# Weight conversion of a two-stage fp32 kernel: a low word's part added in PSUM and a range count on TensorE, fillers in three sizes, a written-out rank for every task

## The chip, the cores and the metric

The kernel runs on one core of one Trainium2 chip. The metric is the device time of one execution in microseconds (us); lower is better. Times of several runs are given as a median with the lowest and the highest.

## The reference

A linear attention without softmax is followed by a two-layer network with a softplus between the layers. All inputs are float32 but the two weights of the network, which come as float64.

```python
kv  = einsum('bhsd,bhse->bhde', k, v)          # 8 batches, 8 heads, s = 576, d = 64
out = einsum('bhsd,bhde->bhse', q, kv)
out = out / sqrt(mean(out * out, axis=-1) + 1e-6) * g_norm
x   = out.transpose(0, 2, 1, 3).reshape(4608, 512)
h   = x @ w_in                                 # 512 x 2048
y   = (maximum(h, 0) + log1p(exp(-abs(h)))) @ w_out   # 2048 x 512
```

## The kernel before

**Precision.** The big products run on TensorE in the reduced type float32r. So each operand (activations x, weights, softplus outputs g) is split into three factors: a high part, the rest scaled by 4096, and a third that corrects their product. Three matmuls then stand for one product. ScalarE makes the high part, VectorE the rest and, for x and g, the third.

**Weights.** The float64 weights arrive as pairs of 32-bit words. `weight` (L410 to L477) takes 512 KB at a time: `c` counts 16 chunks of the 2048 hidden units, and each chunk has an input weight (even j) and an output weight (odd j). VectorE builds a float32 from the high word (`high1` L433, `high2` L437), `mask` (L442) clears what is out of range by help of a square that ScalarE made (L429), `power` (L450) and `rest` (L455) turn the low word into a small float32, and `total` (L459) adds the two. ScalarE's `beyond` (L446) sums how many elements were in range into a column of `over`, from which `whole_scale` derives the scale of the output at L1173. `split_weight` (L486) then makes the three factors: `high` (L496 or L498), `low` (L503 or L506), `low_up` (L509), and for the first four chunks, whose eight weights are needed at once, the third factor goes by TensorE: two matmuls with the identity and the negative identity (`less_by_pe`, L520 and L521) into a PSUM bank, and ScalarE's `third_of_bank` (L524) reads it.

**Attention.** `kv_of` multiplies k and v (small matmuls of 64x64, L691), `rows` turns q on TensorE (L771) or VectorE (L746), multiplies it by kv (L715), squares the result on ScalarE (L788), sums it on VectorE (L719), takes the inverse root on GpSimd (L723), and scales (L727). The first twelve of 36 token tiles are turned by TensorE (L733), the others by VectorE; the first six are split into factors at once (`split`, L635, L638, L641), the others go through DRAM and come back.

**Network.** In the first part a step takes 384 tokens and one chunk: 12 matmuls of 384 columns into a bank (`mm1`, L858), softplus and factors (L880, L882, L869, L873), and nine matmuls of 512 columns for the second layer (`mm2`, L865). In the second part wide steps of 512 tokens take two chunks at once by a scheme with seven products in place of eight (L1060) and 24 matmuls of the second layer (L1130).

**Order.** Nothing of the order is left to a framework. Every piece of work is a task with an engine, an assumed duration, the tasks it follows, buffers it takes and gives back (rings such as `h`, two PSUM banks, `m`, eight SBUF tiles, `raw` and `rawb`, one buffer each for arriving weights), and a due position `pos`. `Plan.order` goes through an assumed time: at each turn it takes, among the tasks that could start soonest, the one with the lowest position, and writes it at the end of its engine's instructions. HANDOVER, READY, SWITCH and LANDING are its assumptions on hand-offs, first starts, changes between kinds of matmuls, and DMAs. Where it foresees at least 400 ns without work for TensorE before the seventh step, it puts a filler there (`warm`, L1224): a matmul of the identity with itself over 512 columns, into a bank of ring `h`, whose result nobody reads. SyncE (SP) issues the DMAs in the order in which the plan lists them.

Of the kernel before, what the change touches and what calls it, by code (L numbers as in the profile page):

```python
# [23 lines left out]
E = 1.0 / RADIX  # L24

# [30 lines left out]
class Plan:  # L56
# [4 lines left out]
    HANDOVER = {"PE": 250, "ACT": 120, "DVE": 120, "POOL": 150, "SP": 0}  # L61
    READY = {"PE": 2500, "ACT": 2500, "DVE": 4000, "POOL": 2500, "SP": 700}
    SWITCH = {("all", "rows"): 90, ("all", "kv"): 90, ("rows", "all"): 250, ("kv", "all"): 250, ("rows", "kv"): 140, ("kv", "rows"): 140}
    TOGETHER, PATIENCE = 1, 0.0
    LANDING, FILLED = 3500, 60000
    KEEP = 4
    BEGIN = 4000
    SOON = 150

# [9 lines left out]
    def add(self, engine, ns, run, after=(), pos=0.0, take=(), give=(), size=0, behind=None, follows=None, kind="all"):  # L79
        pos, behind = round(pos, 4), None if behind is None else round(behind, 4)  # L80
        t = Task(engine, ns, run, [a for a in after if a is not None], pos, list(take), list(give), size)
        for s in t.give:
            s.readers += 1
        self.tasks.append(t)
        t.follows = follows
        t.behind = behind
        t.kind = kind
        return t

    def order(self):  # L90
# [30 lines left out]
        dma_free = 1500  # L121
        last_read = {}
        kind = "all"
        done, left = [], len(self.tasks)
        while left:
            best = None
            for engine, tasks in ready.items():
                options = []
                for t in tasks:
                    at = max(engine_free[engine], t.ready)  # L130
                    if t.size:
                        at = max(at, dma_free - 2500)
# [22 lines left out]
                if engine == "PE" and self.spare and self.spare[-1].start is None:  # L155
                    ring, run, ns, _ = self.spare
                    begin = max(engine_free["PE"], self.BEGIN, min(free[ring])[0] if free[ring] else at)
                    if begin + ns <= at:
                        s = Slot(ring)
                        at, t = begin, Task("PE", ns, lambda s=s: run(s), [], None, [s], [s], 0)  # L160
                        t.kind = "all"
                        s.readers = 1
# [14 lines left out]
            if t.engine == "PE":  # L177
                t.ns += self.SWITCH.get((kind, t.kind), 0)
                kind = t.kind
            t.start = at  # L180
            engine_free[t.engine] = at + t.ns
            t.end = at + t.ns + self.HANDOVER[t.engine]
            if t.size:
                dma_free = max(dma_free, at + t.ns) + t.size
                t.end = dma_free + (self.LANDING if dma_free > self.FILLED else 2000)
# [16 lines left out]
def kernel(  # L202
# [80 lines left out]
    const.tile([P, 8], F32, name="gap0")  # L283
# [125 lines left out]
    def weight(j, pos, fetch_pos, behind):  # L409

        c, of_out = divmod(j, 2)
        raw, w = slot("rawb" if j % 2 and c < 8 else "raw"), slot("m")
        words = 2 if wide else 1
# [7 lines left out]
        f = add("SP", 450, fetch, (), fetch_pos, [raw], size=1800, behind=behind)  # L421
        if wide:
# [30 lines left out]
            def rest():  # L453
                pf = p.tile.bitcast(F32)
                nc.vector.scalar_tensor_tensor(out=pf, in0=words_of()[0], scalar=2.0 ** -52, in1=pf,  # L455
                                               op0=ALU.mult, op1=ALU.mult)

# [7 lines left out]
            d3 = add("DVE", 690, mask, [d2, a1], pos, [])  # L465
            over_done.append(add("ACT", 910, beyond, [d3], pos + (4 if c < 4 else 0), [], [sq]))
# [6 lines left out]
        if c < OWN:  # L473
            divide(j, w, ready, pos, c < 4)
# [4 lines left out]
    def divide(j, w, ready, pos, by_pe=False):  # L479
# [4 lines left out]
        factors_done[of_out, c] = split_weight(w, lambda x: x, d_model, dst, [ready], pos, not of_out, by_pe)  # L484

    def split_weight(w, part_of, n, dst, ready, pos, of_in, by_pe=False):  # L486
# [31 lines left out]
        def less_by_pe():  # L518
            y = new(bank, [P, n])
            nc.tensor.matmul(y, lhsT=ident_r, rhs=dst.tile[:, 0], start=True, stop=False)  # L520
            nc.tensor.matmul(y, lhsT=minus_r, rhs=dst.tile[:, 1], start=False, stop=True)  # L521

        def third_of_bank():
            nc.scalar.activation(dst.tile[:, 2], bank.tile, func=AF.Copy, scale=-E / (1.0 + E))  # L524

# [3 lines left out]
        if by_pe:  # L529
            bank = slot("h")  # L530
            e = add("ACT", 640, low_up, [b], pos, [], [d])
            b2 = add("PE", 500, less_by_pe, [e], pos, [bank])
            e2 = add("ACT", 600, third_of_bank, [b2], pos, [], [bank])
            return [a, e, e2]
# [68 lines left out]
    def load_q(b):  # L603
# [13 lines left out]
        for a in range(4):  # L617
            for p in range(0, NP, 2):
                q_loads[b].append(add("SP", 500, lambda a=a, p=p: run(a, p), (), pos + 0.1 * (2 * a + p // 2),
                                      [q_slots[b]] if not (a or p) else [], [], 1095, behind=pos - 3.5,  # L620
                                      follows=q_loads[b][-1] if a or p else None))

    def split(t, x, ready, pos):
# [20 lines left out]
        a = add("ACT", 640, high, [ready] + ([] if i == 0 else [first_high[n]]), pos, [dst] if i == 0 else [])  # L644
# [17 lines left out]
    def kv_of(b):  # L662
# [7 lines left out]
        for p in range(NP + 1):  # L670
# [4 lines left out]
            def load(src, s, p=p, tail=tail, n=n, ks=ks):  # L675
                if tail:
# [6 lines left out]
                       650 if tail else 850, behind=pos - 5.5) for of_v, (src, s) in enumerate(((k, ks), (v, vs)))]  # L683
# [11 lines left out]
            last = add("PE", 470, run, lds + ([last] if b < 2 else []), pos + 0.5 * p, [bank] if p == 0 else [], [ks, vs], kind="kv",  # L695
# [3 lines left out]
        kv_ready[b] = [add("ACT", 400, lambda: nc.scalar.copy(kvs[b % 2], bank.tile), [last] + o_tasks.get(b - 2, []),  # L699
                           pos + 2.5, [], [bank])]  # L700

    def rows(t):
# [38 lines left out]
        for b, r0, n, s0 in parts(t):  # L741
# [32 lines left out]
            ld = add("SP", 900, load, (), pos - EARLY[7] + P7[20 + t], [q_s] if not at_qa or t == 0 else [], [], 1220 * n // P,  # L774
                     behind=pos - 3.5, follows=first_load[0] if t and at_qa else None)
            first_load.append(ld)
            a = add("PE", 440, turn_q, [ld], pos - 1, [tp], [q_s])
# [482 lines left out]
```

## Time and profile before

| | |
|---|---|
| median of 3 runs | 868.56 us (868.41 to 869.19) |
| span of the profiled execution | 867.5 us |
| TensorE busy | 853.9 us in 6464 matmul records |
| VectorE busy | 704.4 us, 995 instructions |
| ScalarE busy | 521.3 us, 980 instructions |
| GpSimd busy | 76.6 us, 79 instructions |
| first matmul of the network (L858) starts | 44.44 us |
| fillers (L1224) | 52 |
| granted TensorE clock, mean | 1.000 |

A matmul of plain float32 stands in the trace as two records, one of float32r as one. The busy time of a group of matmuls is no measure of what one of them costs, since they overlap; the distance from one start to the next is. All times in the views are from the first instruction of the profiled execution.

### The profile page before, as it was taken

To read this page: it belongs to the slowest core of one execution; us is meant where nothing else is said; L and a number is where in the kernel's file an instruction comes from. 1 tells how busy PE (TensorE), PEld (TensorE's weight loads), DVE (VectorE), ACT (ScalarE), POOL (GpSimd) and SP (SyncE) were. 2 spreads that over 40 slices of the span, in tenths; PEclk is the share of its full clock that TensorE was granted. 3 is DMA by queue.
4 is the path that set the end of the run, shared out by engine and by line. 5 is a ranking of instruction groups with operands and counts; after the bars stand their busy time and mean duration, and the time that the engine had idled before them with its cause. 6 is when DMAs were issued, how large, how long until landed. Compare 5 with 4: busy or idle time off the path is not lost.

```text
span 867.5 us, 17041 instructions
## 1 busy us (share of the span) xinstructions
PE 853.9 (98%) x6464; PEld 760.3 (88%) x6464; DVE 704.4 (81%) x995; ACT 521.3 (60%) x980; POOL 76.6 (9%) x79
## 2 busy tenths in 40 slices
PE   7899999999999999999999999999999999999998
PEld 5678888898888999989999999998999899999996
DVE  7888898888788879798887798878788666788873
ACT  6866664445444467766667655654868555566654
POOL 0342223111113200000000000000000000000000
PEclk9999999999999999999999999999999999999999
DMA  9998998779773655436645546545364752777764
GB/s 278 285 242 230 244 262 255 172 224 234 211 188 114 180 175 166 145 108 209 210 156 164 168 151 205 188 144 170 122 201 140 230 165 91 241 236 241 242 190 126
DMA packets 239778, 167.07 MB, mean 193 GB/s; under 512 B 106320, under 2 KB 198736, under 8 KB 239696
## 3 DMA queue, kind: packets, MB, share of 16 engines
q1 hardware_dynamic: 239392, 165.86, 64.5%
q8 instruction: 50, 0.82, 0.4%
q14 instruction: 32, 0.26, 0.1%
q10 hardware_dynamic: 304, 0.13, 0.1%
HBM read 112.98 MB, written 52.95 MB: 191 GB/s over the span
## 4 chain that ended last, share of the span: by engine, by line
PE 94%; DVE 1%; ACT 1%; POOL 0%; issue 0%; ACTq 0%; DVEq 0%
PE banks L1130 31%; PE banks L1060 28%; PE banks L865 16%; PE banks L858 15%; PE banks L715 2%; PE banks L691 2%; PE banks L733 0%; DVE units L638 0%; DVE half L727 0%; PE banks L1224 0%; POOL roots L723 0%; DVE units L641 0%; DVE roots L719 0%; DVE m L459 0%; ACT units L635 0%
## 5 line engine op out<-in xcount | busy, mean ns | idle before, releaser
L1130 PE MATMUL banks<-pieces,gv 128*128 128x512 f32 x768 | 239.9, 394 | 0.0
L1130 PEld LDWEIGHTS banks<-pieces,gv 128*128 128x128 f32 x768 | 133.5, 189 | 18.4
L1130 PE MATMUL banks<-pieces,g_False 128*128 128x512 f32 x384 | 149.4, 389 | 0.0
L858 PE MATMUL banks<-units,pieces 128*128 128x384 f32 x768 | 145.4, 337 | 0.0
L865 PE MATMUL banks<-pieces,gv 128*128 128x512 f32 x576 | 144.9, 396 | 0.0
L858 PEld LDWEIGHTS banks<-units,pieces 128*128 128x128 f32 x768 | 135.5, 188 | 4.8
L865 PEld LDWEIGHTS banks<-pieces,gv 128*128 128x128 f32 x576 | 106.1, 188 | 20.3
L1060 PEld LDWEIGHTS banks<-units,pieces 128*128 128x128 f32 x840 | 112.8, 190 | 6.8 <-ACT banks L1105 0.4
L1060 PE MATMUL banks<-units,pieces 128*128 128x256 f32 x840 | 117.1, 282 | 0.0
L880 ACT ACTIVATE half<-banks 128x384 f32<-128x384 f32 x64 | 31.4, 491 | 98.2 <-PE banks L858 98.0
L1120 DVE TENSOR_TENSOR gv<-g_True,gv 128x1024 fp32r<-128x1024 f32 x47 | 57.5, 1223 | 37.8 <-ACT gv L1117 37.8
L1130 PEld LDWEIGHTS banks<-pieces,g_False 128*128 128x128 f32 x384 | 72.2, 188 | 15.9
L1060 PEld LDWEIGHTS banks<-units,w 128*128 128x128 f32 x504 | 67.8, 190 | 3.9 <-ACT banks L1105 0.2
L1060 PE MATMUL banks<-units,w 128*128 128x256 f32 x504 | 70.7, 282 | 0.0
L723 POOL TENSOR_TENSOR roots<-roots,half 128x8 f32<-128x8 f32 x36 | 62.3, 1731 | 3.0
L1123 DVE SCALAR_TENSOR_TENSOR g_False<-gv 128x1024 fp32r<-128x1024 f32 x47 | 57.6, 1225 | 1.5
L1109 DVE TENSOR_TENSOR g_True<-banks,g_True 128x512 f32<-128x512 f32 x48 | 33.1, 690 | 30.5 <-PE banks L1060 24.5
L1087 ACT ACTIVATE g_True<-banks 128x256 f32<-128x256 f32 x96 | 36.6, 382 | 32.8 <-PE banks L1060 32.2
L1023 DVE TENSOR_TENSOR units<-loads,units 128x1024 fp32r<-128x1024 f32 x42 | 51.2, 1219 | 6.3 <-ACT units L1020 6.3
L925 ACT ACTIVATE m<-banks 128x512 f32<-128x512 f32 x72 | 42.1, 595 | 19.8 <-PE banks L1130 13.8
L1026 DVE SCALAR_TENSOR_TENSOR units<-units 128x1024 fp32r<-128x1024 f32 x42 | 51.4, 1224 | 1.8
L869 DVE TENSOR_TENSOR gv<-half,gv 128x384 fp32r<-128x384 f32 x64 | 35.4, 553 | 20.6 <-ACT gv L882 19.9
(115 smaller groups left out, 1260.5 us busy)
## 6 DMA issues: line engine op xcount, KB each, us to landing
loads<-x SPq DMA_DIRECT2D x180, 128.0 KB, 2.6
part<-m SPq DMA_DIRECT2D x72, 256.0 KB, 2.9
m<-part SPq DMA_DIRECT2D x72, 256.0 KB, 3.2
loads<-form SPq DMA_DIRECT2D x45, 256.0 KB, 3.2
form<-loads SPq DMA_DIRECT2D x36, 256.0 KB, 3.0
raw<-in_moe_w_in_dram SPq DMA_DIRECT2D x16, 512.0 KB, 4.5
loads<-in_k_dram SPq DMA_DIRECT2D x32, 256.0 KB, 4.1
loads<-in_v_dram SPq DMA_DIRECT2D x32, 256.0 KB, 4.4
```

The source lines that it names most:

```text
L723: nc.gpsimd.tensor_tensor(out=r.tile, in0=r.tile, in1=half, op=ALU.pow)
L858: nc.tensor.matmul(hp, lhsT=w_in.tile[:, i, kd * P:(kd + 1) * P], rhs=xv.tile[:, i, kd], start=(m == 0), stop=(m == 3 * KD - 1))
L865: nc.tensor.matmul(mine[i].tile, lhsT=gv.tile[:, m, i * P:(i + 1) * P], rhs=w_out.tile[:, m], start=(c == cs[0] and m == 0), stop=(c == cs ...
L869: nc.vector.tensor_tensor(out=gv.tile[:, 1], in0=g.tile, in1=gv.tile.bitcast(F32)[:, 0], op=ALU.subtract)
L925: a = add("ACT", 690 if ph == LAST else 600, lambda: nc.scalar.activation(new(ot, [P, d_model]), bank.tile, func=AF.Copy, scale=scale if p ...
L1023: nc.vector.tensor_tensor(out=part_of(1, F32R), in0=xl.tile if m > 1 else xl.tile[:, 0], in1=part_of(0), op=ALU.subtract)
L1026: nc.vector.scalar_tensor_tensor(out=part_of(2, F32R), in0=part_of(1), scalar=-RADIX, in1=part_of(0), op0=ALU.mult, op1=ALU.add)
L1060: nc.tensor.matmul(place(q), lhsT=w[:, m, at:at + P], rhs=dst.tile[:, m, v, kd] if u < 6 else dst.tile[:, m, kd], start=(u == 0 and not m ...
L1087: nc.scalar.activation(dst, src, func=AF.Softplus, scale=1.0 + E)
L1120: nc.vector.tensor_tensor(out=gvt(1, F32R), in0=gt(), in1=gvt(0), op=ALU.subtract)
L1123: nc.vector.scalar_tensor_tensor(out=gt(F32R), in0=gvt(1), scalar=-RADIX, in1=gvt(0), op0=ALU.mult, op1=ALU.add)
L1130: nc.tensor.matmul(mine[i].tile, lhsT=(gvt(m, F32R) if m < 2 else gt(F32R))[:, c, i * P:(i + 1) * P], rhs=outs[c].tile[:, m], start=fresh ...
```

## The change

Four things change.

1. For the first eight weights, `total` is gone. The high factor and the rest `low` are made from the high word's value `t` alone, while the low word's part is written to a buffer of its own (`low_word`, already multiplied by the norm's gain where it is an input weight). TensorE adds the rest and the low word's part in a PSUM bank with two matmuls by the identity. ScalarE's `low_up` reads that bank; the third factor goes by TensorE as before.
2. For the same weights `beyond` is gone. TensorE counts: four matmuls of one column, with the squares as the stationary operand and a tiny constant as the moving one, into a bank; ScalarE reads its one column into `over`.
3. Fillers come in three sizes, 512, 256 and 128 columns, put where the plan foresees 270, 160 or 100 ns without work.
4. The positions are no longer those of the formulas: a list RANK gives each task a rank of its own. The plan's assumptions on durations, hand-offs and DMAs are other numbers as well, and they include how many descriptors and transfers can be under way; they shift where tasks and fillers stand and are no work themselves.

In the order that results, TensorE has 50 fillers of 512 columns, 5 of 256 and 6 of 128.

```diff
+RANK = [
...
-    HANDOVER = {"PE": 250, "ACT": 120, "DVE": 120, "POOL": 150, "SP": 0}
-    READY = {"PE": 2500, "ACT": 2500, "DVE": 4000, "POOL": 2500, "SP": 700}
-    SWITCH = {("all", "rows"): 90, ("all", "kv"): 90, ("rows", "all"): 250, ("kv", "all"): 250, ("rows", "kv"): 140, ("kv", "rows"): 140}
+    HANDOVER = {"PE": 205, "ACT": 140, "DVE": 121, "POOL": 145, "SP": 0}
+    AHEAD = {"PE": 0, "ACT": 107, "DVE": 88, "POOL": 110, "SP": 0}
+    READY = {"PE": 1600, "ACT": 3250, "DVE": 3050, "POOL": 2500, "SP": 700}
+    SWITCH = {("rows", "rows"): 60, ("all", "kv"): 45, ("rows", "kv"): 45, ("rows", "all"): 112, ("kv", "all"): 118}
+    SHARED = ("o", "tp")
...
-    LANDING, FILLED = 3500, 60000
+    ENTRY, LANDING, DESCS, MOVES = 1770, 790, 2560, 8
...
+    WARM = ((270, 4), (160, 2), (100, 1))
...
+        by_pe = wide and c < 4
...
+            def count():
+                y = new(counted, [P, d_model])[:, :1]
+                for i in range(KD):
+                    nc.tensor.matmul(y, lhsT=sq.tile[:, i * P:(i + 1) * P], rhs=few, start=(i == 0), stop=(i == KD - 1))
+
+            def counts():
+                nc.scalar.activation(over[:, j:j + 1], counted.tile[:, :1], func=AF.Identity, scale=2.0 ** -60, bias=much)
...
+            if by_pe:
+                counted = slot("h")
+                cnt = add("PE", 400, count, [a1], pos, [counted], [sq])
+                over_done.append(add("ACT", 200, counts, [cnt], pos, [], [counted]))
+                low_word = slot("m")
+                d4 = add("DVE", 430, power, [d3], pos, [p])
+                d5 = add("DVE", 690, rest, [d4], pos, [low_word], [raw, p])
+                divide_by_pe(j, t, low_word, d3, d5, pos)
+                return
...
+    def divide_by_pe(j, t, low_word, there, rest, pos):
+
+        c, of_out = divmod(j, 2)
+        dst, d, summed, bank = slot("w"), slot("m"), slot("h"), slot("h")
...
+        def total():
+            y = new(summed, [P, d_model])
+            nc.tensor.matmul(y, lhsT=ident_r, rhs=d.tile, start=True, stop=False)
+            nc.tensor.matmul(y, lhsT=ident_r, rhs=low_word.tile, start=False, stop=True)
+
+        def low_up():
+            nc.scalar.activation(dst.tile[:, 1], summed.tile, func=AF.Copy, scale=RADIX)
...
+        a = add("ACT", 640 if of_out else 710, high, [there], pos, [dst])
+        b = add("DVE", 700 if of_out else 750, low, [a], pos, [d], [t])
+        s = add("PE", 500, total, [b, rest], pos, [summed], [d, low_word])
+        e = add("ACT", 600, low_up, [s], pos, [], [summed])
+        b2 = add("PE", 500, less, [e], pos, [bank])
+        e2 = add("ACT", 600, third, [b2], pos, [], [bank])
+        factors_done[of_out, c] = [a, e, e2]
...
-    def warm(s):
+    def warm(s, n):
 
-        nc.tensor.matmul(new(s, [P, 4, P]), lhsT=ident_r, rhs=ident_r.unsqueeze(1).to_broadcast([P, 4, P]),
+        nc.tensor.matmul(new(s, [P, 4, P])[:, :n], lhsT=ident_r, rhs=ident_r.unsqueeze(1).to_broadcast([P, n, P]),
                          start=True, stop=True)
 
-    plan.spare = ("h", warm, 400, mm1s[6][1])
+    plan.spare = ("h", warm, 270, mm1s[6][1])
+    assert len(RANK) == len(plan.tasks)
+    for t, at in zip(plan.tasks, RANK):
+        t.pos = at
```

## The prediction

> **What bounds the kernel now.** I read four views: the page's sums, the time by stretches, TensorE's instructions in order of time, and TensorE's and VectorE's waits up to 62 us.
>
> ```profile
> PE 853.9 (98%) x6464; PEld 760.3 (88%) x6464; DVE 704.4 (81%) x995; ACT 521.3 (60%) x980; POOL 76.6 (9%) x79
> ```
>
> TensorE is idle for 867.5 - 853.9 = 13.6 us. The stretches (length, then busy time and instructions of PE, PEld, DVE, ACT, POOL) say where:
>
> ```profile
> 0.00:5.00 5.00, 3.40 (x8) 2.72 (x9) 2.19 (x9) 1.92 (x2) 0.69 (x6) 1.00 0.59 174
> ...
> 15.00:20.00 5.00, 3.30 (x48) 2.32 (x47) 4.22 (x8) 2.79 (x6) 0.00 (x0) 1.00 1.02 311
> ...
> 40.00:50.00 10.00, 9.16 (x138) 7.48 (x138) 8.68 (x15) 6.17 (x13) 4.12 (x4) 1.00 1.07 235
> ...
> 100.00:150.00 50.00, 50.00 (x596) 44.21 (x593) 44.84 (x77) 28.17 (x56) 16.84 (x16) 1.00 0.87 245
> ...
> 860.00:868.00 8.00, 3.71 (x17) 2.74 (x15) 0.48 (x1) 2.53 (x4) 0.00 (x0) 0.99 0.39 131
> ```
>
> From 80 to 860 us TensorE never stops; there only the number and kind of its matmuls count. 1.6 us of idle lie before its first instruction, 3.8 us behind its last, and 8.2 us in waits up to 80 us. In that first stretch busy is not useful either: 52 fillers (L1224) stand in it. VectorE is busy for 4 to 4.8 us of each 5 there.
>
> ```profile
> 1.60 5.92 PE L1224 MATMUL banks<-ident_r 128*128 128x512 f32 x13 [1.60 <-DVE ident_r L1184]
> 8.27 0.69 PE L691 MATMUL banks<-loads 128*64 128x64 f32 x16 [0.75 <-DMA loads<-in_v_dram]
> ...
> 12.46 1.41 PE L1224 MATMUL banks<-ident_r 128*128 128x512 f32 x5
> 13.70 0.39 PE L520 MATMUL banks<-pieces,ident_r 128*128 128x512 f32 x1
> ...
> 44.44 2.28 PE L858 MATMUL banks<-units,pieces 128*128 128x384 f32 x12
> ```
>
> Columns: start, length, instruction. The first 13 fillers take 5.92 us, 0.455 each; the five at 12.46 take 13.70 - 12.46 = 1.24, about 0.24 each. The first matmul of the main work (L858, "first mm1" below) starts at 44.44; 867.5 - 44.4 = 823.1 us follow it. So the time is the start of the first mm1, plus TensorE's work behind it, plus what still waits there.
>
> **Prices, from starts in the trace.** A 512-column matmul in a dense run takes 0.231 (nine L865 from 255 to 257: 2.08), with a filler's pause 0.235; transposes 0.10 each. The small products of the attention cost more by their visits than by themselves:
>
> ```profile
> 266.83 0.69 PE L715 MATMUL banks<-early,w 64*64 64x64 f32 x32
> 267.46 2.36 PE L865 MATMUL banks<-pieces,gv 128*128 128x512 f32 x9
> ...
> 278.11 1.16 PE L715 MATMUL banks<-early,w 64*64 64x64 f32 x64
> 279.20 1.65 PE L865 MATMUL banks<-pieces,gv 128*128 128x512 f32 x6
> ```
>
> From the L858 at 264.63 to the one at 269.66 are 5.03 us, of which 2.10 + 2.08 are the big matmuls' own: 0.85 for one group of L715. The visit at 278.11 has two groups and costs by the same sum 1.28. So a group is 0.43 and a visit as such 0.42, because the big matmuls on either side are about 0.1 longer and the pipeline is refilled. A group of L691 is 0.45; going from L691 straight to L715 costs 0.14.
>
> **The change, part by part.**
>
> *Low word added in PSUM* (eight weights; the new order does have eight L459 fewer). VectorE loses eight L459 of 0.69 = 5.5 us; TensorE gains 8 x 2 matmuls = 16 x 0.235 = 3.8 us. L509's scaling now reads PSUM; L524, which does so already, takes 0.60 against L509's 0.63, so nothing.
>
> *Range counted by TensorE.* ScalarE gives up 0.72 + 0.19 and takes a one-column reading, between the 0.19 of L446's accumulator and the 0.35 of a 256-column copy (L699): some 5 us saved on an engine that is 60% busy, nothing on the path. TensorE gains 32 weight loads with one-column matmuls. None is in this trace. Lower end: a record of the one-column L1173 starts 0.028 behind the other, 4 x 0.028 = 0.1 a weight; upper end: four loads of 0.188 that nothing hides (PEld's mean) and four times 0.028, 0.9. The nearest rows are the 128x128 transposes, 0.10 each with their load; a count has no 128 columns to stream, so I take a little less than four of them, 0.3 a weight, 2.4 in all (0.8 to 7).
>
> *Fillers.* The new order has 50 of 512 columns, 5 of 256, 6 of 128: 12.7 us against 52 x 0.235 = 12.2. So 0.5 more; the smaller sizes take no time out, they only fill gaps that stood open before.
>
> *New ranks.* From 300 us on the order of TensorE's instructions is nearly the old one. In front it differs: attention visits go from 32 to 46, and direct L691-L715 passages from 11 to 4: 14 x 0.42 - 7 x 0.14 = 4.9 us more.
>
> Together TensorE gets 3.8 + 2.4 + 0.5 + 4.9 = 11.6 us more. What can pay for it: the 8.2 us of waits, some 0.13 more at each of about 20 waits (the last matmul's drain, which counts as busy: a lone filler is listed with 0.40 to 0.51) = 2.6, and a part of the 13 - 7 slow fillers.
>
> *Up to the first mm1.* The new order lists for TensorE: fillers 50, 4 and 5 of the three sizes 12.5; counts 7 x 0.3 = 2.1; 28 matmuls of the weights 6.6; L691 ten groups 4.5; 44 transposes 4.4; L715 five groups 2.2; 15 visits 6.3. With 1.6 at the start and 7 slow fillers' extra 1.5 this is 41.7. The same list for the old order gives 35.7 against 44.44, so 8.7 were waits. VectorE's list from the first weight's landing (4.36, unchanged) to the third token tile's last factor has 55 operations: 14 of 0.46, 41 of 0.61 to 0.73, 34 us, so 38.3. Two waits in it stay. The second input weight needs its predecessor's buffer and the SP queue has as many issues in front of it as before; it was read first at 13.79, and VectorE is now through with the first two by 12.2: 1.6. The first reduction stands behind the first L715, which follows on TensorE almost as late as before (VectorE began it at 23.30 after a wait of 0.72); VectorE is now there by about 21: 2.4. So 42.3, and with smaller hand-offs 43.7 for the first mm1. TensorE had been late in the old order as well: its six fillers ran at 42.96 when the third tile was done at 40.7.
>
> *Behind it.* Old remainder 823.1. More: 10 visits 4.2, one L715 group and two times four transposes 1.2, a count 0.3; less: two weight matmuls 0.5, fillers 0.3, six passages 0.8: +4.1. The old remainder holds 1.5 us of idle and its drains; VectorE has less to do, so I take 0.5 of it off. 43.7 + 823.1 + 4.1 - 0.5 = 870.4. The profiled execution's span was 867.5 where the median of the runs is 868.56, 1.1 more: **871.5**.
>
> What covers what: the eight additions and the counts lie where TensorE has fillers, but the new order does not have fewer fillers, so their 6 us are paid for by waits that go, and only by those. Each weight takes three banks of ring h in turn where it took one, of two that mm1 and the fillers use too; SUM waits for ScalarE to empty one. If that cover is gone a weight costs one PSUM reading, 0.6, more: up to 4.8.
>
> One rule weighed. The 13 fillers start 0.43 apart to the last at 6.89; later ones 0.235. The Trainium skill, "TensorE: Matmul & The Clock Gate", Part 1, says that the clock is released only after some 3.4 us of sustained work. The trace agrees. Now the first seven fillers end near 4.8 and the count behind them waits for a square that ScalarE ended at 5.04. By the trace alone the pause means nothing; if the pause defers full speed, the next eight fillers take 0.2 longer each, 1.6 us, and the first addition comes at 9.1 instead of 8.5.
>
> **Rivals.**
> - *All waits close* (faster). Place: TensorE before the first mm1, and its idle up to 80 us. If VectorE's two waits vanish, TensorE's own list decides, 41.7, and no wait follows: 41.7 + 823.1 + 4.1 - 2.5 = 866.4, and with the counts at their lower end 1.6 less: 864.8, as a median 865.9. It decides once VectorE's list ends before 41.7. For: VectorE loses 5.5 us just there. Against: its waits are for DMA and TensorE. 0.13.
> - *Small visits are cheaper near the start and counts lie under other loads*: half of the 4.2 and 1.6 of the counts go, 871.5 - 3.7 = 867.8, no change that can be told. 0.27.
> - *Old waits return as new ones.* TensorE waited 3.5 us for k and v; DMA is at 1.0 and over from 5 to 40 us. Loads are reordered; if these come again on top, 875; with banks of h short, 877. 0.15.
> - *The slow clock's 1.6 us reach the first mm1*: 873. 0.08.
> - The forecast, 869.5 to 873: 0.37.
>
> **The numbers.** 0.2% of 868.6 is 1.7 us, about what a measurement of this kernel can tell from no change. Faster (under 866.8) 0.13; within (to 870.3) 0.27 and a tenth of the forecast's part, 0.30; slower 0.57. Range 866.9 to 876.5: the upper end takes in the first of the two prices of the third rival.
>
> **What would show it.** TensorE's idle up to 80 us at 4 to 6 us instead of 8.2; first mm1 between 43 and 45; 16 additions at 0.23 to 0.24; a count of four at 0.2 to 0.4; no idle from 100 to 860 us and a remainder of 826 to 828. A first mm1 below 42, or a remainder at 823, would prove me wrong.

## The result and the profile after

The changed kernel takes **872.79 us** (median of 5 runs, 872.68 to 875.11); the kernel before took 868.90 in the same series (868.41 to 871.24). The ratio is **1.0044**, 95% interval 1.0031 to 1.0056: slower by 3.9 us, where 871.5 was forecast. The profiled execution is the longest of the five (875.11, span 873.3; the other four have spans of 870.9 to 871.2), so its own surplus of some 2.3 us has to be kept apart from what the change does.

The page's sums, in the layout of those shown of before, and its chain by engine:

```profile
PE 863.7 (99%) x6521; PEld 766.3 (88%) x6521; DVE 695.7 (80%) x989; ACT 516.1 (59%) x972; POOL 77.2 (9%) x80
...
PE 94%; DMA 3%; DVE 1%; POOL 1%; ACT 1%; SPq 0%; issue 0%; DVEq 0%; ACTq 0%
```

TensorE is busy 9.8 us longer, VectorE 8.7 us less, ScalarE 5.2 us less. The work did move as the diff says, onto the engine that was the bound, and nothing of what VectorE and ScalarE gave up shows in the time.

The stretches (length, then busy time and instructions of PE, PEld, DVE, ACT, POOL, then the clock, the DMA share, GB/s):

```profile
15.00:20.00 5.00, 4.95 (x26) 3.56 (x26) 3.48 (x6) 3.55 (x7) 0.00 (x0) 1.00 1.05 352
...
40.00:50.00 10.00, 9.95 (x135) 7.82 (x136) 6.81 (x12) 6.02 (x13) 3.86 (x4) 1.00 0.86 199
...
100.00:150.00 50.00, 48.10 (x634) 41.31 (x634) 44.55 (x78) 28.70 (x56) 16.98 (x18) 1.00 0.94 252
```

TensorE is fuller up to 50 us than before (4.95 of 5 from 15 to 20, where it had 3.30), and yet that buys nothing. From 100 to 150 us it has 1.9 us of idle that before did not have. TensorE's waits from 75 to 160 us name it:

```profile
PE banks L917 <- DMA loads<-in_v_dram: 2.5, 2, 1.9
```

These two waits for v do not come in every execution: e2 and e9 below, with the same order of loads from there on, had no idle in that stretch, and e5 had one such wait of 1.9.

TensorE in order of time, from the start to the first addition, and the first matmul of the network (L1084, formerly L858):

```profile
1.61 3.35 PE L1453 MATMUL banks<-ident_r 128*128 128x512 f32 x7 [1.61 <-DVE ident_r L1410]
5.48 0.27 PE L639 MATMUL banks<-rest_of,sq 128*128 128x1 bf16 x4 [0.52 <-ACT sq L606]
5.61 4.16 PE L1453 MATMUL banks<-ident_r 128*128 128x512 f32 x10
9.56 0.73 PE L697 MATMUL banks<-m,ident_r 128*128 128x512 f32 x1
...
45.99 2.20 PE L1084 MATMUL banks<-units,pieces 128*128 128x384 f32 x11
```

Seven fillers, the count's wait of 0.52, then ten more fillers at 0.4 each: still half clock. Full speed was granted at 11.0 us (before: 7.6). **The first mm1 is 1.55 us later than before** (45.99 against 44.44). The last thing that it needs, the third factor of the third token tile, leaves VectorE at 44.95 (L867; before: L641 at 40.73), and TensorE, which is never idle from 41.3 us on, comes to the first mm1 1.04 later. VectorE's waits up to 47 us (total, times, longest):

```profile
DVE m L610 <- DMA raw<-in_moe_w_in_dram: 5.2, 2, 3.6
DVE roots L945 <- ACT half L1014: 2.2, 1, 2.2
DVE ident_r L1410 <- POOL early masks.py:199: 1.3, 1, 1.3
DVE half L953 <- PE banks L941: 1.2, 1, 1.2
DVE m L632 <- POOL rest_of L1413: 0.4, 1, 0.4
```

The first two are the waits that the prediction kept, both bigger or later than it said. The first attention output and the first reduction, in after (L941, L945) and in before (L715, L719), and the last factor in after:

```profile
24.82 0.69 PE L941 MATMUL banks<-early,w 64*64 64x64 f32 x32
26.20 0.69 DVE L945 TENSOR_REDUCE roots<-half 128x8 f32<-128x512 f32 x1 [2.16 <-ACT half L1014]
44.26 0.69 DVE L867 SCALAR_TENSOR_TENSOR units<-units 128x512 fp32r<-128x512 f32 x1
```

```profile
21.44 1.16 PE L715 MATMUL banks<-early,w 64*64 64x64 f32 x64
23.30 1.28 DVE L719 TENSOR_REDUCE roots<-half 128x8 f32<-128x512 f32 x2 [0.72 <-ACT half L788]
```

The first reduction starts at 26.20, where before's started at 23.30. From there to the first mm1 are 19.8 us, before 21.1: the chain behind it is 1.3 shorter, but it starts 2.9 late.

Where the time lies between landmarks of the main work, from starts on TensorE (mm1 counted by its matmuls; us):

| | to first mm1 | to the 121st | to the 241st | to the 481st | to the end |
|---|---|---|---|---|---|
| before | 44.4 | 59.8 | 49.7 | 96.9 | 616.7 |
| after, profiled | 46.0 | 57.5 | 53.9 | 98.3 | 617.6 |
| e2 below | 46.4 | 56.5 | 51.9 | 98.3 | 617.4 |
| e9 below | 45.7 | 56.7 | 51.9 | 98.3 | 618.7 |

After is ahead of before at the 121st mm1 (103.5 against 104.2) because nine mm2 matmuls fewer stand in front of it (72 for 81). It pays behind: from the 121st to the 241st stand 256 records of attention output and 160 of k-v where before had 192 and 112. From the first mm1 to the 481st e2 needs 206.8 and before 206.4, of which 1.5 were idle.

### The profile page after: what moved, and what is told of

Same layout as the page of the kernel before. It is cut to its first block, busy times and chain, and to the rows that moved or that the text cites. A ratio compares the mean times of both kernels' runs of the same rounds, so it can differ in the third digit from the quotient of the medians.

```text
span 873.3 us, 17113 instructions
## 1 busy us (share of the span) xinstructions
PE 863.7 (99%) x6521; PEld 766.3 (88%) x6521; DVE 695.7 (80%) x989; ACT 516.1 (59%) x972; POOL 77.2 (9%) x80
## 4 chain that ended last, share of the span: by engine, by line
PE 94%; DMA 3%; DVE 1%; POOL 1%; ACT 1%; SPq 0%; issue 0%; DVEq 0%; ACTq 0%
PE banks L1356 30%; PE banks L1286 28%; PE banks L1084 14%; PE banks L1091 14%; PE banks L917 2%; PE banks L941 2%; DMA loads<-in_v_dram 2%; PE banks L1453 1%; POOL roots L949 1%; DMA m<-x 1%; DMA raw<-in_moe_w_in_dram 0%; PE banks L959 0%; PE banks L997 0%; DVE half L953 0%; PE banks L697 0%
## 5 line engine op out<-in xcount | busy, mean ns | idle before, releaser
L1356 PEld LDWEIGHTS banks<-pieces,gv 128*128 128x128 f32 x768 | 133.1, 189 | 18.7 <-DVE banks L1130 0.8
L1091 PE MATMUL banks<-pieces,gv 128*128 128x512 f32 x576 | 146.5, 397 | 0.0
L1084 PE MATMUL banks<-units,pieces 128*128 128x384 f32 x768 | 146.4, 338 | 0.0
L1084 PEld LDWEIGHTS banks<-units,pieces 128*128 128x128 f32 x768 | 134.9, 188 | 4.9
L1091 PEld LDWEIGHTS banks<-pieces,gv 128*128 128x128 f32 x576 | 105.5, 188 | 20.0
L1346 DVE TENSOR_TENSOR gv<-g_True,gv 128x1024 fp32r<-128x1024 f32 x47 | 57.5, 1223 | 37.3 <-ACT gv L1343 37.2
L1335 DVE TENSOR_TENSOR g_True<-banks,g_True 128x512 f32<-128x512 f32 x48 | 33.0, 688 | 36.9 <-PE banks L1286 26.4
L1249 DVE TENSOR_TENSOR units<-loads,units 128x1024 fp32r<-128x1024 f32 x42 | 51.2, 1219 | 10.2 <-ACT units L1246 10.1
L1246 ACT ACTIVATE units<-loads 128x1024 fp32r<-128x1024 f32 x42 | 44.4, 1057 | 14.7 <-PE banks L1286 12.1
```

Source lines behind the costliest of these rows:

```text
L1084: nc.tensor.matmul(hp, lhsT=w_in.tile[:, i, kd * P:(kd + 1) * P], rhs=xv.tile[:, i, kd], start=(m == 0), stop=(m == 3 * KD - 1))
L1091: nc.tensor.matmul(mine[i].tile, lhsT=gv.tile[:, m, i * P:(i + 1) * P], rhs=w_out.tile[:, m], start=(c == cs[0] and m == 0), stop=(c == cs ...
L1246: nc.scalar.activation(part_of(0, F32R), xl.tile if m > 1 else xl.tile[:, 0], func=AF.Copy, scale=DOWN)
L1249: nc.vector.tensor_tensor(out=part_of(1, F32R), in0=xl.tile if m > 1 else xl.tile[:, 0], in1=part_of(0), op=ALU.subtract)
L1346: nc.vector.tensor_tensor(out=gvt(1, F32R), in0=gt(), in1=gvt(0), op=ALU.subtract)
L1356: nc.tensor.matmul(mine[i].tile, lhsT=(gvt(m, F32R) if m < 2 else gt(F32R))[:, c, i * P:(i + 1) * P], rhs=outs[c].tile[:, m], start=fresh ...
```

## The experiments

Several kernels change only the emitted order. Numbers in them are tasks in the order in which the kernel makes them: 0 to 14 are the first weight's tasks, 30 to 44 the third one's, which is the second input weight (load, square, high1, high2, mask, count, reading of the count, ...), 380 to 393 the first k-v sum, 394 to 401 the first token tile from q load to norm. The helper is the same in all:

```python
order = plan.order()

def move(i, before):
    t, u = plan.tasks[i], plan.tasks[before]
    order.remove(t)
    order.insert(order.index(u), t)
```

Each kernel was timed against the kernel before on the same chip: e1 to e4 beside 868.93, e5 to e8 beside 869.75, e9 to e11 beside 869.07, e12 beside 868.75 us. Theories at the start: TensorE's extra work is the loss (mine), against late loads, fillers in the way (rival A) and the clock (rival B).

### e1: no fillers

```diff
 for t in plan.order():
-    t.run()
+    if t.pos is not None:
+        t.run()
```

> The changed kernel in its own order of instructions, with all 61 fillers left out (nothing reads them). Theory (TensorE's own list is the bound up to the first mm1, and fillers stand ahead of work that is ready): the first mm1 comes at 42 to 44 us instead of 46.0, and the time falls by 2 to 4 us to 869 to 871. Rival A (fillers fill only real waits): first mm1 at 46, 872.8. Rival B (without fillers the clock stays at half in the first 40 us): the work ahead of the first mm1 takes up to twice as long per matmul, first mm1 at 47 to 50, 874 to 877.

Measured: 876.54 us, ratio 1.0080 (1.0049 to 1.0111); first mm1 at 51.7. The clock was full from 17.4 to 20.8 only, half to 27.6, full to 41.3, half to 51.5. The stretches (clock in the column behind POOL):

```profile
12.00:17.00 5.00, 5.00 (x29) 3.58 (x29) 1.56 (x4) 2.00 (x5) 0.00 (x0) 1.00 0.98 290
17.00:22.00 5.00, 1.93 (x22) 1.25 (x23) 3.07 (x6) 3.72 (x8) 0.00 (x0) 0.88 1.01 294
22.00:27.00 5.00, 5.00 (x50) 3.39 (x46) 3.44 (x6) 1.71 (x3) 0.00 (x0) 0.50 0.79 230
```

The 3.07 us without TensorE's work in the second row are followed by half speed in the third. What follows: fillers are not free time thrown away; without them the clock falls and the first mm1 comes 5.7 us later, so rival B holds for the kernel without fillers, with a first mm1 still later than its 47 to 50.

### e2: the first 17 fillers only

```diff
+fillers = 0
 for t in plan.order():
-    t.run()
+    fillers += t.pos is None
+    if t.pos is not None or fillers <= 17:
+        t.run()
```

> The changed kernel in its own order with only the first 17 fillers (up to the first addition); the 44 later ones are left out. Theory: the start is as before, at 18 to 21 us TensorE is ahead by the 16 fillers that stood there (3.8 us) and waits for data instead; first mm1 at 43 to 45, 870 to 872. Rival A (fillers fill only real waits): 46 and 872.8. Rival B (clock): the pauses let the clock fall, first mm1 later than 46.

Measured: 872.33 us, 1.0039 (1.0026 to 1.0053), first mm1 at 46.44, idle up to there 12.9 us against 3.3. At the median, 44 fillers less change the first mm1 by 0.5 us and the time by nothing that can be told. That does not show that fillers delay nothing, for the clock moved too. In the profiled execution it was half from 18.1 to 24.9, as rival B expected, and the ten executions come in the order of their mean granted clock: four with 0.998 took 871.46 to 871.70 us, three with 0.996 took 872.23 to 872.61, and three with 0.994 to 0.989 took 873.59 to 876.09. The first four are faster by about 1 us or more than every execution of after (872.68 and up). So the fillers seem to cost about what the clock that they hold up saves; the two were not measured apart. TensorE's waits up to 47 us show what the fillers had covered:

```profile
PE banks L639 <- ACT sq L606: 5.4, 4, 2.3
PE banks L697 <- DVE m L690: 1.6, 2, 1.5
```

5.4 us in front of counts (L639) that wait for squares. VectorE's wait for the load was 3.5, for the first reduction 2.9: TensorE's list is not what VectorE waits for first. Behind the first mm1 TensorE has no idle at all, and that remainder is 824.1.

### e3 and e4: conversion alone, order alone

e3 is the kernel before with the new conversion of the first eight weights (parts 1 and 2 of the change) and its own positions; e4 is the kernel after without the list of ranks. In both, loads of tasks at very early positions are let off one of the plan's reserves of buffers.

```diff
-                        if engine == "SP" and s.ring in ("m", "n"):
+                        if engine == "SP" and s.ring in ("m", "n") and t.pos > -40:
...
-    assert len(RANK) == len(plan.tasks)
-    for t, at in zip(plan.tasks, RANK):
-        t.pos = at
```

> The kernel before with the new conversion alone (addition and count on TensorE), in the old plan with its formulas, its assumptions and its one filler size; the reserve of ring m no longer holds back the loads of x, as the plan does not come out otherwise. 39 fillers instead of 52, 38 attention visits instead of 32. Theory (what TensorE gets more must be paid by waits): +6.2 of additions and counts, -3.1 of fillers, +2 of visits, and VectorE's 5.5 us less shorten the waits of 8.7 by about as much: 867 to 870. Rival (the additions and counts themselves are the loss): 872 and more.

> The changed kernel without the list of ranks: new conversion, new assumptions and three sizes of fillers, positions by the old formulas (the reserve of ring m as in the run of the conversion in the old plan). 55 fillers of 512, 6 of 256, 8 of 128 columns, 39 visits. Theory (more fillers and additions on TensorE are the loss, whatever orders them): 872 to 875. Rival (the ranks, with 46 visits, are the loss): 868 to 870.

Measured: 899.16 (1.0341, 1.0312 to 1.0370) and 893.25 (1.0268, 1.0244 to 1.0293); none of the expectations explains this (the rival's "872 and more" in e3 is met only as a number). e3 has 18.7 us of idle behind the first mm1, 7.4 of them between 300 and 400 us, and e4 11.6. I take it that the conversion's tasks take other buffers and durations, and that the old formulas for positions fall out of step far behind the eight weights; this was not tested, and the reserve, let off in both runs and not in after, may have its part. So neither prices a part; they only show that the conversion in the old positions is far slower. e8 looks at it from the other side.

### e5 and e6: the second input weight's load first

```diff
+move(30, 394)
 for t in order:
     t.run()
```

e6 is the same with the 17 fillers of e2. In after, SP issues that load at 11.81 us (before: 9.61), behind four q loads that hold SP for 3.52 us.

> The changed kernel in its own order, but the load of the second input weight goes ahead of the four q loads that stand in front of it in SyncE's queue. In the changed kernel it is issued at 11.81 us and VectorE waits 3.55 us for it; now it should be issued at about 8.5 and read at 13. Theory (VectorE's wait for that load, which is longer by 2 us than forecast, is what made the first mm1 late): together with the fillers behind it TensorE still starts the first L941 at about 24 to 25, so only a part comes through: first mm1 44 to 46, 870.5 to 872.8. Rival (the load is not the cause, TensorE's own list is): unchanged at 46.0 and 872.8.

> The same, and only the first 17 fillers are kept, so that TensorE isn't held at 16 to 20 us by 16 fillers. Theory: both covers are gone, VectorE's list moves up by about 3 us, the first mm1 comes at 43 to 44 and the time is 869 to 870. Rival (TensorE's list or a later load decides anyway): as with 17 fillers alone, 46.4 and 872.3.

Measured: e5 874.14 (1.0048, 1.0031 to 1.0065), first mm1 45.73, one v wait of 1.9 as in the profile of after; e6 873.17 (1.0047, 1.0026 to 1.0067), first mm1 48.8, clock half at 19.6 to 26.4 and 40.0 to 46.9. VectorE in e5:

```profile
12.88 0.43 DVE L610 TENSOR_SCALAR m<-raw 128x512 uint32<-128x512 uint32 x1 [0.17 <-DMA raw<-in_moe_w_in_dram]
13.34 0.69 DVE L614 SCALAR_TENSOR_TENSOR m<-raw,m 128x512 uint32<-128x512 uint32 x1
17.22 0.69 DVE L619 SCALAR_TENSOR_TENSOR m<-sq,m 128x512 f32<-128x512 bf16 x1 [3.19 <-ACT sq L606]
```

The wait for the load shrinks from 3.55 to 0.17, and a wait of 3.19 for ScalarE's square stands two instructions later: ScalarE has its q copies in front. The load was a wait, not the cause.

### e7: the first count behind the ten fillers

```diff
+move(5, 11)
+move(6, 11)
```

> The changed kernel with the first weight's count put behind the 17 fillers, so that these run without a pause from 1.6 us on, as the 13 of the kernel before do. Theory (the pause at 4.96 kept the clock at half until 11.0 instead of 7.6): full clock at about 7.6 again, the first addition at 8.6 instead of 9.56; but as VectorE waits for the second input weight until 16.2 anyway, the first mm1 stays at 46 and the time at 872 to 873. Rival (the slow first 11 us are the loss): first mm1 earlier by 1 to 2 us, 871.

Measured: 874.02 (1.0050, 1.0034 to 1.0066), first mm1 47.95. Full speed came at 6.0, earlier than in after. The fillers then ended early, TensorE waited 1.6 us for the first addition, and the clock was half again from 9.4 to 16.2. Early full speed was lost to a pause.

### e8: the new ranks, the old conversion

The eight weights take the kernel before's tasks (`total`, `beyond`, no count, no addition on TensorE) in the places of the new ranks, with 17 fillers.

```diff
-        by_pe = wide and c < 4
+        by_pe = False
...
+                f, a1, d1, d2, d3, cnt, counts, d4, d5, a, b, s_, e, b2, e2 = r
+                r = [f, a1, d1, d2, d3, counts, d4, d5, min(a, b) - 0.5, a, b, e, b2, e2]
```

> The changed kernel with the old conversion (total on VectorE, beyond on ScalarE, no addition or count on TensorE), its tasks in the given ranks, and only 17 fillers, to be compared with the changed kernel with 17 fillers (872.3, first mm1 46.4). Theory (VectorE is the bound up to the first mm1, so the new conversion is worth its time there): seven L459 of 0.69 more stand in VectorE's list, less what falls into its waits, first mm1 at 48 to 51, 874 to 877. Rival (the additions and counts on TensorE cost as much as they save): 871 to 873.

Measured: 877.21 (1.0085, 1.0070 to 1.0100), first mm1 47.17. Beside e2 (1.0039), which differs in the conversion and in what the plan makes of it, this is 0.46% more, about 4 us. So under these ranks, and with 17 fillers, the new conversion is not what costs time. The 4 us are no price of VectorE's work, though. The first mm1 is only 0.7 later than in e2, and the clock differs: after its first full speed e8 ran 17.1 us at half (from 17.3, 30.9 and 48.0 us), e2 6.8. At like clocks the two are close: e8's two executions with 0.990 took 875.99 and 876.62, e2's with 0.992 and 0.989 took 874.75 and 876.09. Most of the difference thus goes with the clock. Whether the old conversion pulled the clock down was not tested, nor was this version with all its fillers.

### e9 and e10: the load and its square first

```diff
+move(30, 394)
+move(31, 27)
```

e10 adds two moves (`move(62, 399)`, `move(63, 399)`: two steps of VectorE's on the next weight ahead of the first reduction) and leaves out fillers 26 to 36. Nothing reads a filler's result.

> As the run with the second input weight's load first, and ScalarE's square of that weight goes ahead of the reading of the first output weight's sum, because in that run VectorE lost its wait for the load and got one of 3.2 us for the square, which stood behind two copies of q. Theory (VectorE's list decides, but only as far as TensorE is not held by the 16 fillers at 16 to 20 us): VectorE's waits for load and square are gone, those for the first reduction grow to about 5 us, first mm1 at 45 to 46, 871.5 to 873. Rival (VectorE's waits at 13 to 17 us alone make the first mm1 late): first mm1 at 43, 869 to 870.

> The same, and 11 of the 16 fillers at 16 to 20 us are left out, and VectorE's first two operations on the third input weight go ahead of the first reduction. Theory: the load, the square, the fillers and the reduction each held the next; with all four taken away the chain moves up by 2 to 3 us, first mm1 at 43 to 44, 869 to 870.5. Rival (the loads of k, v and q, or a lower clock, take their place): first mm1 at 45.5 to 46.5 and 872 to 873.

Measured: e9 873.25 (1.0045, 1.0031 to 1.0058), first mm1 45.74; e10 872.66 (1.0037, 1.0023 to 1.0051), first mm1 46.53. VectorE's waits in e9:

```profile
DVE m L692 <- ACT pieces L685: 2.7, 1, 2.7
DVE m L610 <- DMA raw<-in_moe_w_in_dram: 2.3, 2, 2.1
DVE roots L945 <- ACT half L1014: 2.2, 1, 2.2
```

Load and square are now in time (0.15 of wait at 13.23), and the third wait in a row takes their place: L692 waits for the high factor L685, which ScalarE has behind its reading of a count that TensorE has behind fillers. The first reduction stays put: its wait is 2.2 as in after. e10 removes those fillers; the wait for L685 is still 2.66, the reduction comes at 26.75 (e9: 25.95), and the clock falls for 3.4 us at 20.8. So its rival held. In e9 the clock was full from 5.4, and the first addition came at 9.48 after a wait for VectorE:

```profile
9.48 0.50 PE L697 MATMUL banks<-m,ident_r 128*128 128x512 f32 x1 [0.87 <-DVE m L692]
```

In after, at half clock, it came at 9.56. The slow clock at the start cost it at most 0.1.

### e11: the kernel before without its six last fillers

```diff
+    fillers += t.pos is None
+    if t.pos is not None or not 45 <= fillers <= 50:
+        t.run()
```

> The kernel before, with the six fillers (42.96 to 44.44 us) just ahead of its first mm1 left out. Theory (the old plan's fillers stood in front of work that was ready: the third tile's last factor was done at 40.7): first mm1 at 43.0 to 43.3, and since TensorE is the bound behind it the time falls by up to 1.3 us, less what returns as waits behind it: 867.3 to 868.5 against 868.6. Rival (the six fillers covered a wait): no change, first mm1 at 44.4.

Measured: 868.92, ratio 0.9999 (0.9986 to 1.0011): the same. The first mm1 starts at 42.88, 1.56 earlier than before:

```profile
42.25 0.69 PE L715 MATMUL banks<-early,w 64*64 64x64 f32 x32 [0.62 <-ACT half L788]
42.88 1.32 PE L858 MATMUL banks<-units,pieces 128*128 128x384 f32 x6
```

The remainder grows from 823.0 to 824.4, with 2.28 us of idle instead of 1.49. **An earlier first mm1 is given back**, at least for the most part: it is not by itself the measure that the prediction took it for. A gain of some tenths is not excluded: the eight executions with a granted clock of 0.999 or more have a median of 868.46, before's twelve in the same series 868.97.

### e12: the first attention output first

My last theory: counts that wait for squares, fillers and an addition stand ahead of the first attention output (L941, at 24.82 in after; before's L715 at 21.44) in TensorE's one order, and make the first reduction late. Besides e9's moves and e10's missing fillers:

```diff
+for i in (386, 389, 392):
+    move(i, 35)
+move(393, 36)
+move(397, 50)
+move(398, 51)
+move(399, 49)
```

> The kernel after with its own work and another order of it: the second input weight's load and its square first, as in e10, eleven fillers (the 26th to 36th) less; and on TensorE the products that end the first k-v sum (L917) and the first attention output (L941) now stand ahead of the counts of the third and fourth weight, with their copy and square ahead of those weights' on ScalarE and the first reduction ahead of the fourth weight's on VectorE. Nothing reads the fillers that are left out. My theory (the later first mm1 comes from the place of the first attention output behind counts that wait for squares, in TensorE's one order): first L941 at 19.5 to 21.5 us instead of 24.8, first reduction at 21.5 to 23 instead of 26.2, first mm1 at 42.5 to 44 instead of 46.0, remainder 824.5 to 826, so 868.5 to 871.5 and at most 1.003 times the kernel before. Rival 1 (loads decide: k and v for this sum do not land earlier): L941 waits for a DMA, first reduction not before 25, first mm1 45.5 to 46.5, 872 to 873. Rival 2 (VectorE's sum of work decides, the place of one reduction does not matter): the reduction moves to 22 to 23 but a wait of 2 to 3 us comes up on VectorE elsewhere before the first mm1, which stays at 45.5 to 46.5; 872 to 873.

Measured: 875.92, ratio 1.0076 (1.0063 to 1.0089), first mm1 at 49.88: the theory fell. TensorE:

```profile
19.41 0.69 PE L917 MATMUL banks<-loads 128*64 128x64 f32 x16 [1.67 <-DMA loads<-in_k_dram]
21.14 1.12 PE L917 MATMUL banks<-loads 128*64 128x64 f32 x16 [1.05 <-DMA loads<-in_v_dram]
22.02 1.09 PE L917 MATMUL banks<-g 128*64 128x64 f32 x16
23.05 0.27 PE L639 MATMUL banks<-rest_of,sq 128*128 128x1 bf16 x4
23.67 1.13 PE L941 MATMUL banks<-early,w 64*64 64x64 f32 x32 [0.36 <-ACT early L925]
```

The mechanism of rival 1 showed, with a first mm1 and a time well above its 45.5 to 46.5 and 872 to 873: k and v for this sum were not there before 19.4 and 21.1. And the copy of that sum (L925), moved forward on ScalarE, blocked what stands behind it there. VectorE:

```profile
15.99 0.75 DVE L632 SCALAR_TENSOR_TENSOR m<-raw,rest_of,m 128x512 fp32r<-128x512 uint32 x1
24.33 0.75 DVE L692 SCALAR_TENSOR_TENSOR m<-m,g_col,pieces 128x512 fp32r<-128x512 f32 x1 [7.59 <-ACT pieces L685]
```

7.59 us of wait, the largest new one of all runs, and half clock from 21.0 to 27.9. In after, the counts and the fillers stood where TensorE would otherwise have waited for k and v. In before, the last k load of this sum is issued at 12.21 and the v loads at 10.65; in e12 these loads leave SP at 14.17 to 16.08, in after at 13.01 to 14.97. The order of the loads, not TensorE's, bounds the first output in e12; how much of the 3.4 us between 21.44 and 24.82 it takes in after itself was not measured alone. An order with those k and v loads ahead of the q loads was not tried.

## Why the prediction was right

Its sign and its main reason held: TensorE is the bound, it got more work, and closed waits paid for part of it. The forecast sum was +2.9 us; +3.9 was measured. Of the 1.3 us between 871.5 and 872.79, 0.6 lie in the span (870.4 against 871.0), and the rest in the step from span to time, for which the forecast added 1.1, while each of after's five executions takes 1.8 more than its span. Step by step:

| step | forecast | measured in after |
|---|---|---|
| addition, two matmuls | 2 x 0.235 | 0.34 + 0.23 from start to start (13.62, 13.96, 14.19); 5.1 for all eight, the first of them at half clock, where 3.8 was forecast |
| one count of four | 0.3 (0.1 to 0.9) | 0.12 (18.28 to 18.40); 1.1 for all eight, where 2.4 was forecast |
| waits of TensorE up to 80 us, without the 1.6 at the start | 4 to 6 | 1.7 |
| load wait on VectorE | 1.6 | 3.55 |
| wait of the first reduction | 2.4 | 2.16 |
| VectorE done with the third tile | 42.3 | 44.95 |
| first mm1 | 43.7 | 45.99 |
| remainder | 826.7 | 827.3; in e2 and e10, without the v waits, 824.1 and 824.7 |

*The first mm1 is the term that was off*, by 2.3 us. VectorE was done 2.65 later than its list said, and the rows account for 2.5 of it: the first weight landed 0.39 later (4.75, not "4.36, unchanged"), a wait of 0.42 for GpSimd came up, the load's wait was 1.95 longer, and the first reduction's 0.24 shorter. "The SP queue has as many issues in front of it as before" failed: 14 stand in front of the load, where before had 12, and it was issued 2.2 later. The two more are q loads of half the size, 1.36 us together; the four whole ones hold SP for 3.52, 0.6 of it in waits for earlier loads to land, and before's four for 3.35. And at the first reduction VectorE was not "there by about 21" but at 24.0; the first output stood at 24.82, 3.4 later than before's, not "almost as late as before". Yet e5 and e9 took the load's wait away and gained 0.25 us at the first mm1: it is one of a row of waits, each with the next one close behind. The forecast's method, VectorE's list plus two waits, does not show such a row. Two of its readings were off without effect: the nine L865 of 2.08 run from 252.91, and the DMA share was 0.93, not 1.0 and over, from 25 to 30 us.

*The remainder was forecast too high* by about as much. Its +4.1 of work was +2.6 in e2 (824.1 with no idle, against 823.0 - 1.5 of before) and +3.3 in after itself (827.3 - 2.5). Added up from start to start, without idle, after's +3.3 divides so. Up to the first wide step, the small products together with the big matmuls around them (L917, L941, L1084, L1091) take +3.0, where 3.8 was forecast (4.2 + 0.4 - 0.8); the transposes +0.8, as forecast; the weights' matmuls, additions and counts -0.9, where -0.2 was forecast; the fillers -0.5, where -0.3 was. The wide part behind takes +0.9, for which the forecast had nothing. So two errors of some 2 us, in the first mm1 and behind it, cancelled, and that the span came within 0.6 us is luck. How the executions of after without v waits divide their 871.0 cannot be seen, since only one has a trace; if their first mm1 also stood at 46.0, their remainder was 825.0.

*What covers what* fits: TensorE's waits up to 80 us went from 8.2 to 1.7, and the eight additions and counts take about 6. That the one paid for the other was not tested by itself. ScalarE's and VectorE's savings do not show in the sum of before against after; what they are worth under the new ranks e8 leaves open, because the clock differs.

The rivals. *All waits close*: they nearly did, 1.7 us of them are left up to 80 us, and no time was gained, because 61 fillers and earlier work stood in them; e2 shows 12.9 us of idle with about the same time, part of it at half clock. Idle that vanishes is no gain unless the last thing waited for comes sooner. *Cheaper visits and counts*: the counts are cheap, 0.12 for 0.3, and the remainder was lower; the first mm1 hid it. Visits and groups behind the first mm1 took 0.8 less than forecast in all, but where a visit can be read as in before, at 264.17, its two groups cost 1.28, as at 278.11 of before. *Old waits return*: the profiled execution had 2.5 us of waits for v and is 2.3 longer than the rest; not the median. They lie at 95 and 127 us, and before's waits for k and v lay in front of 40. *The slow clock*: its mechanism happened. Full speed came at 11.0 instead of 7.6; the rule of the Trainium skill ("TensorE: Matmul & The Clock Gate", Part 1), that full speed needs some 3.4 us of sustained work, agrees with it in so far as the pause of 0.52 at 4.96 was followed by late full speed; the last section shows executions in which full speed came before a longer pause was over. Its price of 1.6 us did not reach the first mm1, because the first addition waits for VectorE until about 9.5 at either clock (e9).

What stays open: that the loss is TensorE's added work and the later start rests on the sums of two traces, as no run changed one of them alone and got the time back. Open too is an order in which the first reduction comes at 23 with the new conversion, and what that would be worth. e11 says little: 1.56 us earlier at the first mm1 brought nothing in the kernel before. No version tried beats the kernel before.

## What to carry to other kernels

Work taken off engines that are not the bound and put on the one that is has to be paid for by waits of that engine, and a wait counts only if nothing else stands close behind it: here a load, a square, a factor, and the loads of k and v came up one after the other, each as the last was removed. Count a queue's issues one by one, and with their times. Before the first landmark of the main work is taken as the measure, test whether an earlier landmark shortens the whole: removing six fillers moved it by 1.56 us and the time by nothing that could be told. And before two kernels that pause differently are compared, look at the clock that each execution was granted: in e2 the times follow it.

## What the runs showed of the hardware

The clock goes up and down in steps of 3.4 us: records of half or full speed in these runs last 3.4, 6.8, 10.2 or 13.7 us, or longer multiples. I cut the first 60 us of each execution into pieces of 3.41 us that end where its clock changes, and summed TensorE's busy time in each piece:

| piece | TensorE busy in 3.41 us |
|---|---|
| at full speed, followed by half speed (11 pieces, in e1, e2, e6, e7, e8, e10, e12) | 0.45 to 1.90 |
| at full speed, followed by full speed (all runs) | from 1.96 up |
| at half speed, followed by full speed | 2.82 (e2), else 3.01 to 3.41 |
| at half speed, followed by half speed | up to 2.95, and some with 3.01 to 3.41 (e1, e6, e7, e8) |

In these 60 us the fall goes with the busy time: after at most 1.90 of 3.41, some 56%, the clock falls, and after 1.96 it stays. Further on this does not hold: the pieces from 127.1 us in after, with 1.51, and from 126.3 in e5, with 1.54, were followed by full speed, and e3 and e4 have four more, with 1.53 to 1.95. So 1.90 is no threshold, though all falls up to TensorE's last matmul, the five later ones of e3 and e4 too (0.47 to 1.69), came after pieces with at most that. The Trainium skill, "TensorE: Matmul & The Clock Gate", Part 1, lets half speed return after an idle window; here it returned after windows that were not idle, five of the eleven with TensorE busy for over half, so the measurement decides. The rise cannot be read off in the same way. After's own piece from 4.2 to 7.6 us had 2.90 and did not raise the clock; e2's first had 2.82 and did. In before and after the pieces happen to lie alike, so these two can be compared: before's piece from 4.2 to 7.6 had 3.33 and raised the clock, after's, with the pause in it, did not. In other executions the pieces begin elsewhere: with the same seven fillers from 1.61 us, full speed came at 11.0 in after with a pause of 0.52 behind them and at 10.6 in e10 with 1.21, but at 5.4 in e9, inside its pause of 0.97, and at 4.4 in e2, before its pause of 1.07 began. So the length of the pause does not order them. That the pieces lie on a grid that does not start with the kernel is my reading of these records, not a test.

Four q loads in a row held SP for 2.2 (e10) to 4.0 us (after), waits for earlier loads included, where a load of k or v mostly takes 0.4 to 0.5; a queue's order is a cost of its own.
